# A planner that keeps apart only the streaming parts of operations at a shared port, and a GpSimd that waits one VectorE operation earlier

## The chip, the cores and the metric

The kernel runs on one core of one Trainium2 chip. The metric is device time in microseconds of one execution, as a median over runs. The engines are named as the profile names them: PE (TensorE), ACT (ScalarE), DVE (VectorE), POOL (GpSimd), SP (SyncE, which only issues DMAs here).

## The reference

Two layers, each of attention and a feed-forward block, over 2048 rows of width 448 in bf16, with residuals:

```python
def _A_ref(x, wqkv, wo):                       # H = 16 heads, Dh = 28
    q, k, v = (x @ wqkv) split into heads
    scores = jnp.einsum("bhqd,bhkd->bhqk", q, k) * scale
    p = _softmax(scores, axis=-1)
    return (p @ v, heads joined) @ wo
def _B_ref(x, w1, b1, w2, b2):                 # F = 1792
    h = x @ w1 + b1
    return jnp.where(h > 0, h, 0) ** 2 @ w2 + b2
x = x + _A_ref(_layernorm(x), ...)
x = x + _B_ref(_layernorm(x), ...)
x = x + _A_ref(_layernorm(x), ...)
x = x + _B_ref(_layernorm(x), ...)
```

The costly part is the softmax: 2 layers x 16 heads x 2048 x 2048 exponentials, with no subtraction of a maximum.

## The kernel before

**Tiles.** Queries are taken in blocks of 256 rows (the last two blocks of the second layer have 128), heads in groups of four. A *unit* is one head, one query block and as many key blocks as make a 128x512 tile of scores: 2048 units in all. `s_stream` (matmuls at line 993) multiplies keys with queries into a PSUM tile `sc` that holds three units; there are two such tiles. `e_stream` (line 1023) lets ScalarE take the exponential of the tile into `pt`. `p_stream` (line 1179) multiplies `pt` with the values `V_sb` and accumulates in `oT`; a column of ones in `V_sb` gives the sum of the softmax. Around it run the projections (line 721, evacuated at 740 to 772), the layer norms (562, 567, 589 and 590 on GpSimd, 684, 631), the normalisation of the attention's output (1206, 1208, 1288, 1307, or 1249 to 1265), the output projection with the residual (1317) and the feed-forward block (relu at 1375, square at 1384).

**Units that ScalarE does not do.** `apart` decides, when a tile of scores is issued, whether its third unit is handed to VectorE and GpSimd. Then ScalarE's instruction has 1024 columns instead of 1536, and the unit takes this way (`a_unit`, `a_rest`), where the exponential is built from integer parts and a parabola:

- `take`, line 1071, VectorE, PSUM to an SBUF buffer `v_w` (or a corner of `K_sb`);
- `part`, line 1088, GpSimd, the fraction of the exponent into `pd`, which is the unit's place in `pt` or a spare buffer in `V_sb`, `h` or `pd`;
- `bend`, line 1094, VectorE, squares it;
- either `whole`, line 1100, GpSimd, the integer part, and then `close`, line 1109, VectorE, adds the two in 16 bit; or `close` in one float operation, line 1118, VectorE alone.

`apart` says yes only where a buffer is free and where VectorE's queue of work, as the planner sees it, is under `PACE[step]`; the choice between 1109 and 1118 goes by `MIXT[step]`. Both are lists of 128 numbers, one for each 128th of the units.

**What sets the order.** The program's order on each engine is fixed when the kernel is built. A `Planner` holds some dozens of streams, each with a priority and a next operation (`Op`) with an estimated duration. It places at every step the operation that can start first by its estimates. On the chip each engine runs its instructions in that order, each waiting for semaphores of what it depends on. VectorE and GpSimd share a port to SBUF. An `Op` with `port=True` uses it: lines 684, 1094, 1109, 1118, 1384, 1307 on VectorE, 589/590, 1088, 1100 on GpSimd. This is how `earliest` keeps them apart (a and b are the start and end of an operation of the other engine, x the operation itself):

```python
for a, b, x in self.ports["POOL" if e == "DVE" else "DVE"]:
    if e == "DVE" and a <= s < b:
        s = b
    elif e == "POOL" and s < b and a < s + dur:
        s, after = b + PSYNC, x
```

So in the plan a VectorE operation starts when GpSimd's has ended, and the other way round. For a GpSimd operation that was put behind x the program also gets a true wait for the end of x (`behind`). For VectorE there is no such wait: on the chip it runs on, and the port decides.

Of the kernel before, what the change touches and what calls it, by code (L numbers as in the profile page):

```python
# [27 lines left out]
PENB = 0.3  # L28
# [4 lines left out]
PX = -9  # L33
# [41 lines left out]
C_PRIO = 1.6  # L75
V_PRIO = 8.5
# [17 lines left out]
PACE = (1.4, 4.0, 1.0, 3.4, 1.4, 1.4, 1.4, 1.0, 3.0, 1.0, 2.6, 1.4, 4.0, 2.2, 1.8, 3.0, 1.4, 4.0, 1.4, 1.8, 1.4, 4.0, 3.0, 3.0, 1.8, 3.0, 2.6, 2.2, 1.8, 3.0, 4.0, 1.4, 1.8, 3.4, 2.2, 3.0, 3.0, 4.0, 2.2, 3.0, 0.6, 2.6, 3.0, 1.4, 4.0, 4.0, 2.2, 3.0, 1.4, 3.0, 3.4, 2.6, 0.6, 2.6, 2.6, 0.6, 1.8, 2.2, 1.4, 2.2, 1.8, 1.8, 2.2, 4.0, 1.8, 3.0, 1.8, 2.2, 4.0, 3.4, 1.8, 2.6, 3.4, 3.4, 2.6, 1.8, 2.2, 3.4, 4.0, 3.4, 3.0, 4.0, 3.4, 3.4, 4.0, 3.0, 2.6, 1.4, 3.4, 1.8, 2.2, 1.8, 3.4, 3.4, 0.6, 3.4, 2.6, 1.0, 1.8, 2.2, 2.6, 3.4, 0.6, 2.6, 3.4, 3.4, 1.0, 2.2, 3.0, 2.2, 2.2, 2.6, 1.8, 3.0, 3.0, 3.0, 2.6, 3.0, 2.2, 3.0, 3.0, 1.4, 2.6, 2.2, 2.6, 2.6, 2.6, 2.6)  # L94
MIXT = (-9.0, 1.2, 99.0, 99.0, -9.0, -9.0, -9.0, -9.0, 1.8, -9.0, -9.0, 1.2, 1.2, 1.8, -9.0, 1.8, -9.0, 1.2, -9.0, 1.2, -9.0, 1.8, 1.2, 1.2, -9.0, 1.8, 1.2, -9.0, 1.2, -9.0, 99.0, 1.8, 1.2, 1.2, -9.0, -9.0, -9.0, 1.2, 1.8, 1.2, -9.0, 1.2, 1.8, -9.0, 1.8, 1.2, 1.2, 1.2, -9.0, 1.2, -9.0, 1.8, -9.0, 1.2, 1.8, 99.0, -9.0, 1.2, -9.0, -9.0, 1.8, 1.2, -9.0, -9.0, -9.0, -9.0, -9.0, -9.0, 1.8, -9.0, 1.8, 1.2, -9.0, 1.8, 99.0, -9.0, 1.8, 1.2, -9.0, 1.8, 1.8, 99.0, 99.0, 99.0, 99.0, 1.2, -9.0, 99.0, 1.8, 1.8, 1.2, -9.0, 1.8, -9.0, 1.2, -9.0, 1.8, -9.0, 1.8, 1.2, 1.8, -9.0, -9.0, -9.0, 99.0, 1.8, -9.0, -9.0, 1.2, 1.2, 1.8, 1.8, -9.0, -9.0, 1.2, -9.0, 1.2, 1.8, 1.8, 1.8, 1.2, -9.0, 1.8, 1.2, 99.0, 99.0, 99.0, 99.0)
# [44 lines left out]
class Op:  # L140
    __slots__ = ("eng", "dur", "fn", "deps", "acq", "rel", "mode", "sets", "start", "end", "res", "turn", "ready", "lat", "need", "got", "more", "room", "port", "base", "w", "after", "ins", "durs")

    def __init__(self, eng, dur, fn, deps=(), acq=None, rel=None, mode="full", sets=(), lat=0.0, need=1, port=False):
# [7 lines left out]
        self.w = self.after = self.ins = self.durs = None  # L151
# [5 lines left out]
class Planner:  # L157
# [3 lines left out]
    def __init__(self):  # L161
        self.clock = {"PE": 0.0, "ACT": 0.0, "DVE": 0.0, "POOL": 0.0, "DMA": 0.0, "-": 0.0}
        self.mode = None
        self.tok = {}
        self.streams = []
        self.past = {"PE": [], "DVE": []}
        self.used = []
        self.ports = {"POOL": [], "DVE": []}
        self.turns = lambda: False
        self.slack = lambda: SLACK  # L170

    def behind(self, late, soon):
# [18 lines left out]
    def earliest(self, o):  # L191
# [20 lines left out]
        for e in o.eng:  # L212
# [16 lines left out]
    def run(self):  # L229
        while self.streams:  # L230
# [14 lines left out]
            free = min((c[0] for c in known if c[2] == "DVE" and not c[3][2].port and c[3][2].dur > 0.2), default=1e9)  # L245
            pool = min((c[0] for c in known if c[2] == "POOL" and c[3][2].port), default=1e9)
            locked = min((c[0] for c in known if c[2] == "DVE" and c[3][2].port), default=1e9)

            def key(c):
# [4 lines left out]
                return c[0] + (PENB if held else PENA if wait else 0.0), c[1]  # L254
# [20 lines left out]
            if o.port and e in self.ports:  # L275
                self.ports[e] = [*self.ports[e][-5:], (s, o.end, o)]
# [16 lines left out]
def kernel(  # L293
# [134 lines left out]
    def sums():  # L428
# [20 lines left out]
        def split(e):  # L449
            nc.vector.tensor_copy(out=cs[:, 0:NFC], in_=box["t"][:, 0:NFC])  # L450
            nc.vector.tensor_tensor(out=cs[:, NFC:2 * NFC], in0=box["t"][:, 0:NFC], in1=cs[:, 0:NFC], op=ALU.subtract)
# [50 lines left out]
    def wprep():  # L502
        def cp(dst, c0, h0, h1):
            def fn(e):
# [4 lines left out]
                else:  # L509
                    nc.vector.tensor_copy(out=d, in_=src)  # L510
# [46 lines left out]
    def stats(mv, t0, j, deps, src=None, rel=None):  # L557
        box = {}

        def take(e):  # L560
            box["st"] = sp.tile([P, 6], DT.float32, name="st")
            nc.vector.bn_stats(out=box["st"][:, :], in_=x_sb[:, t0 + j, :] if src is None else src())  # L562

        def merge(e):
            if mv[0] is None:
                mv[0] = sp.tile([P, 4, 2], DT.float32, name="mv")
            nc.vector.bn_aggr(out=mv[0][:, j, :], in_=box["st"][:, :])  # L567
# [5 lines left out]
    def layernorm(t0, nt, deps_of, early=False, mv=None, place=None, x_in=None, parts=False):  # L573
# [9 lines left out]
        for a, b in [(0, 1), (1, 2)] if single else [(0, nt)]:  # L583
# [8 lines left out]
            rs = Op("POOL", 0.95, rsqrt, deps=[mv[1][b - 1]], sets=[("rs", t0 + a)] if early else (), port=True)  # L592
            rss += [rs] * (b - a)
            pl.spawn(EV, iter([rs]))
            if not parts and NORMG and not early:
                def turned(e, a=a, b=b):
                    ln["m"] = mv[0][:, 2:4, 0]
                    nc.vector.tensor_scalar(out=ln["m"][:, a:b], in0=mv[0][:, a:b, 0], scalar1=-1.0, scalar2=None, op0=ALU.mult)
# [12 lines left out]
        def turn(p0, own, xs):  # L611
# [13 lines left out]
            def ev(e, p0=p0, w=len(xs) * P):  # L625
# [4 lines left out]
                else:  # L630
                    nc.vector.tensor_copy(out=dst, in_=tp[:, :, 0:w])  # L631
# [4 lines left out]
        if parts:  # L636
# [4 lines left out]
            for lo, hi in ((0, 2 * P), (2 * P, D)):  # L641
                def norm(e, lo=lo, hi=hi):
                    nc.vector.tensor_scalar(out=xn[:, lo:hi], in0=x_sb[:, t0, lo:hi],
# [6 lines left out]
            for h, nm in enumerate(nms):  # L650
# [11 lines left out]
                def ev(e, h=h):  # L662
                    nc.vector.tensor_copy(out=xnT[:, 2 * h:2 * h + 2, 0:P], in_=box["t"][:, 2 * h:2 * h + 2, 0:P])
# [6 lines left out]
        for p0 in range(0, nt, wide):  # L670
# [4 lines left out]
            for j in js:  # L675
# [12 lines left out]
                nm = Op("POOL" if on else "DVE", GN if on else 0.39, norm, deps=[rss[j], *([] if x_in is None else [x_in])], sets=[("n", t0, j)] if early else (), port=True)  # L688
# [45 lines left out]
    def copy_to(dst, by=None):  # L734
        def f(e, t):
# [3 lines left out]
            elif by is not None:  # L739
                nc.vector.tensor_scalar(out=dst, in0=src, scalar1=by, scalar2=None, op0=ALU.mult)  # L740
            elif e == "ACT":
                nc.scalar.copy(out=dst, in_=src)
            else:
                nc.vector.tensor_copy(out=dst, in_=src)
        return f

    def qkv(l, t0, nt, xnT, own_xt, ends, early=False):
# [13 lines left out]
        def values():  # L761
            nonlocal last
            for tb in range(t0, t0 + nt):
                if l == 1:
                    yield Op("POOL", 0.2, lambda e, tb=tb: nc.gpsimd.memset(V_sb[1][:, tb, :, DH:DHP], 1.0))
                def evv(e, t, tb=tb):
# [4 lines left out]
                    else:  # L771
                        nc.vector.tensor_copy(out=o, in_=i)
# [99 lines left out]
    step = [0]  # L872
# [54 lines left out]
    def s_stream():  # L927
        while at[0] < len(units):
# [5 lines left out]
            def fn(e, gi=gi, us=us, js=js):  # L934
# [19 lines left out]
                else:  # L954
# [18 lines left out]
                    pl.spawn(C_PRIO, a_unit(gi, x, dst[-1], us[-1], passes[us[0][0]][0]))  # L973
# [90 lines left out]
    def a_unit(gi, x, src, unit, l):  # L1064
# [3 lines left out]
        def take(e):  # L1068
# [4 lines left out]
            if x is gbuf[gi]["s"]:  # L1073
                apart_from(gi, t)
        c = Op("DVE", 0.69, take, deps=[("s", gi)], acq=sets_of(unit), rel=x)
# [3 lines left out]
        pl.spawn(lambda now: V_LAST if e_now[1] - gi >= V_AGE or at[0] > ends_at[unit[0]] + V_PAST else V_LATE if now > c.end + V_WAIT else V_PRIO if gi > FIRST else V_FIRST, a_rest(gi, c, box, unit))  # L1079

    def a_rest(gi, c, box, unit):
# [7 lines left out]
        y = Op("POOL", GY, part, deps=[c, ("p", gi)] if own else [c], acq=None if own else lambda: pd_free(unit), port=True, lat=YL)  # L1089
# [5 lines left out]
        h = Op("DVE", 0.42, bend, deps=[y], port=True)  # L1095
        gbuf[gi]["x"] = y
        if left[0] > MIXT[step[0]]:
# [3 lines left out]
            z = Op("POOL", GZ, whole, deps=[y], port=True, lat=YL)  # L1101
# [8 lines left out]
            yield Op("DVE", 0.42, close, deps=[h, z], rel=c, sets=("x", gi), port=True, lat=XL)  # L1110
# [9 lines left out]
        yield Op("DVE", 0.683, close, deps=[h], rel=c, sets=("x", gi), port=True, lat=XL)  # L1120
# [7 lines left out]
    def p_stream():  # L1128


        for pi, (l, qb, g, kbs, first, last) in enumerate(passes):
# [65 lines left out]
            def ev(e, box=box, first=first, last=last, g=g, res=res, n=n, l=l, qb=qb):  # L1197
# [7 lines left out]
                if first:  # L1205
                    nc.vector.tensor_copy(out=dst, in_=src)
                else:
                    nc.vector.tensor_tensor(out=dst, in0=src, in1=part(l, qb, g), op=ALU.add)
# [30 lines left out]
    def norm_turn(l, qb, g, oe, pass_box):  # L1239
# [7 lines left out]
        def turn(e):  # L1247
            box["t"] = rp.tile([P, 2, QR], DT.float32, name="rec")
            nc.vector.transpose(out=box["t"][:, 0, 0:n], in_=pass_box["t"][:, 0:n])
# [3 lines left out]
        def rcp(e):  # L1253
            box["r"] = sp.tile([P, QR // DHP], DT.float32, name="rq")
            nc.vector.reciprocal(out=box["r"][:, 0:n // DHP], in_=halves(box["t"][:, 0, 0:n])[:, :, DH])
# [405 lines left out]
```

## Time and profile before

| | |
|---|---|
| Median of 3 runs | 826.27 us (825.02 to 827.38) |
| The profiled execution's own time | 825.07 us |
| Its span, first to last instruction | 823.3 us |
| Mean granted clock of TensorE | 0.992 |
| Busy: PE / DVE / ACT / POOL | 778.8 / 771.6 / 803.8 / 387.2 us |

A group row of the profile reads: line, engine, operation, what it writes and reads, shapes, count, then busy time and mean duration in ns, then the idle time just before, with who ended it. A window row gives busy time and count for PE, weight loads, DVE, ACT and POOL, then the granted clock, the DMAs' share and GB/s. A timeline row gives start, duration and the instruction.

### The profile page before, as it was taken

What the parts mean: (1) busy time and instruction counts of PE and PEld (TensorE: products, weight loads), DVE (VectorE), ACT (ScalarE), POOL (GpSimd) and SP (SyncE); (2) the same over time, 40 slices, a digit from 0 to 9 for tenths busy, and PEclk for the clock granted to TensorE, in tenths of its full rate; (3) what the DMA queues carried; (4) which work ended last, traced back from release to release, by engine and by line L of the source; (5) the groups of instructions that cost most, each with busy time, mean ns of one, the idle gap of its engine ahead of it and who ended that gap; (6) DMA issues with size and microseconds to landing.
All of it is one profiled execution on the core that took longest, in us unless ns stands there. A gap on an engine that the chain in (4) does not pass through costs nothing.

```text
span 823.3 us, 27379 instructions
## 1 busy us (share of the span) xinstructions
PE 778.8 (95%) x11410; PEld 402.7 (49%) x11410; DVE 771.6 (94%) x1722; ACT 803.8 (98%) x699; POOL 387.2 (47%) x654
## 2 busy tenths in 40 slices
PE   8999999999999999999999999988999999999997
PEld 4444545444545444454444544434454544445665
DVE  6999999999999999999999999899999999999965
ACT  7999999999999999999999999999999999999994
POOL 3244554655554465545445436344644545465500
PEclk9999999999999999999999999799999999999999
DMA  9200000000000000000000000011000000000000
GB/s 257 70 2 2 21 24 15 15 16 16 4 13 15 16 15 16 9 9 15 2 2 2 2 2 3 11 35 29 27 16 21 21 27 27 10 20 15 21 14 13
DMA packets 32364, 17.92 MB, mean 22 GB/s; under 512 B 17833, under 2 KB 31787, under 8 KB 32240
## 3 DMA queue, kind: packets, MB, share of 16 engines
q1 hardware_dynamic: 32240, 16.18, 7.0%
q8 instruction: 89, 1.46, 0.7%
q14 instruction: 35, 0.29, 0.1%
HBM read 13.88 MB, written 2.07 MB: 19 GB/s over the span
## 4 chain that ended last, share of the span: by engine, by line
ACT 34%; PE 30%; DVE 24%; issue 10%; POOL 1%; DMA 0%; ACTq 0%; DVEq 0%; POOLq 0%
ACT pt L1023 34%; PE mt L721 13%; PE sc L993 10%; PE oT L1179 5%; DVE v_w L1071 4%; DVE r L1375 3%; DVE pt L1109 2%; DVE pt L1094 2%; DVE x_sb L1317 1%; DVE K_sb L1071 1%; DVE st L562 1%; DVE V_sb L1109 1%; DVE V_sb L1094 1%; DVE V_sb L1384 1%; PE sc L721 1%
## 5 line engine op out<-in xcount | busy, mean ns | idle before, releaser
L1023 ACT ACTIVATE pt<-sc 128x1536 bf16<-128x1536 f32 (+1 forms) x683 | 793.0, 1374 | 3.8 <-PE sc L993 3.1
L993 PE MATMUL sc<-Q_sb,K_sb 32*128 32x256 bf16 (+1 forms) x4436 | 279.7, 267 | 29.2 <-ACT pt L1023 20.8
L993 PEld LDWEIGHTS <-K_sb 32*128 32x128 bf16 x4436 | 107.8, 92 | 205.3 <-issue 135.0
L1100 POOL TENSOR_SCALAR v_w<-v_w 128x512 int16<-128x512 f32 x191 | 121.3, 635 | 94.0 <-DVE pt L1109 25.0
L1179 PE MATMUL oT<-pt,V_sb 128*32 128x256 bf16 (+1 forms) x3996 | 157.3, 270 | 0.9 <-ACT pt L1023 0.5
L1071 DVE TENSOR_SCALAR v_w<-sc 128x512 f32<-128x512 f32 x213 | 144.8, 682 | 6.5 <-PE sc L993 5.3
L721 PE MATMUL mt<-xnT,w 128*128 128x256 bf16 (+1 forms) x896 | 119.7, 271 | 4.1 <-DVE xnT L631 1.9
L1179 PEld LDWEIGHTS <-V_sb 128*32 128x32 bf16 x4352 | 89.9, 96 | 54.7 <-issue 44.8
L721 PEld LDWEIGHTS <-w 128*128 128x128 bf16 x896 | 75.0, 97 | 39.1 <-issue 30.4
L1088 POOL TENSOR_SCALAR pt<-v_w 128x512 bf16<-128x512 uint16 x94 | 58.8, 626 | 51.0 <-PE sc L993 9.5
L1375 DVE TENSOR_SCALAR r<-mt 128x512 bf16<-128x512 f32 x108 | 73.5, 682 | 4.4 <-PE mt L721 4.2
L1088 POOL TENSOR_SCALAR V_sb<-v_w 128x512 bf16<-128x512 uint16 x75 | 46.3, 617 | 55.0 <-DVE V_sb L1109 12.8
L721 PE MATMUL mt<-w,V_sb 128*128 128x448 bf16 (+1 forms) x274 | 69.0, 353 | 0.0
L1100 POOL TENSOR_SCALAR K_sb<-K_sb 128x512 int16<-128x512 f32 x72 | 46.0, 639 | 36.9 <-DVE h L1109 6.2
L1071 DVE TENSOR_SCALAR K_sb<-sc 128x512 f32<-128x512 f32 x84 | 57.3, 682 | 4.1 <-PE sc L993 3.3
L1094 DVE TENSOR_TENSOR pt<-pt 128x512 bf16<-128x512 bf16 x130 | 57.7, 459 | 1.1 <-POOL pt L1088 1.1
L589 POOL TENSOR_TENSOR ve<-mv,eps_t 128x2 f32<-128x2 f32 (+1 forms) x33 | 6.4, 194 | 77.1 <-DVE mv L567 39.7
L1094 DVE TENSOR_TENSOR V_sb<-V_sb 128x512 bf16<-128x512 bf16 x93 | 40.1, 435 | 0.5 <-POOL V_sb L1088 0.5
L1317 DVE TENSOR_TENSOR x_sb<-x_sb,mt 128x448 bf16<-128x448 bf16 x61 | 37.2, 610 | 3.3 <-PE mt L721 3.2
L1109 DVE TENSOR_TENSOR pt<-pt,v_w 128x512 int16<-128x512 bf16 x88 | 38.8, 451 | 1.1 <-POOL v_w L1100 0.2
L562 DVE BATCH_NORM_STATS2 st<-x_sb 128x6 f32<-128x448 bf16 x63 | 38.4, 615 | 1.1 <-DMA x_sb<-in_A_x_dram 0.7
L1088 POOL TENSOR_SCALAR pt<-K_sb 128x512 bf16<-128x512 uint16 x36 | 22.3, 618 | 32.7 <-DVE K_sb L1071 6.4
(151 smaller groups left out, 925.3 us busy)
## 6 DMA issues: line engine op xcount, KB each, us to landing
rec<-scr SPq DMA_DIRECT2D x54, 128.0 KB
x_sb<-in_A_x_dram SPq DMA_DIRECT2D x8, 224.0 KB
out_dram<-x_sb SPq DMA_DIRECT2D x15, 112.0 KB
w<-in_B_w_dram SPq DMA_DIRECT2D x1, 1568.0 KB
w<-in_B_w_dram SPq DMA_DIRECT2D x1, 1344.0 KB
dn<-oT_sb SPq DMA_DIRECT2D x54, 4.0 KB
V_sb<-in_A_wqkv_dram SPq DMA_DIRECT2D x4, 168.0 KB
scr<-dn SPq DMA_DIRECT2D x27, 8.0 KB
```

The costliest lines, as they stand in the source:

```text
L562: nc.vector.bn_stats(out=box["st"][:, :], in_=x_sb[:, t0 + j, :] if src is None else src())
L721: nc.tensor.matmul(box["t"][:, c0:c0 + n], lhsT=lhsT() if callable(lhsT) else lhsT, rhs=rhs, start=a, stop=b)
L993: nc.tensor.matmul(dst[k][:, i * nt * P:(i + 1) * nt * P], lhsT=K_sb[l][rows, g, (kb + i) * P:(kb + i + 1) * P], rhs=Q_sb[rows, g, t0 * P: ...
L1023: t = nc.scalar.activation(out=pt[:, 0:n], in_=gbuf[gi]["sc"][:, 0:n], func=AF.Exp, scale=float(np.log(2.0)) * 2.0 ** -FRAC)
L1071: t = nc.vector.tensor_scalar(out=box["w"], in0=two(src), scalar1=EXP_SHIFT, scalar2=EXP_LOW, op0=ALU.add, op1=ALU.max)
L1088: return nc.gpsimd.tensor_scalar(out=two(pd), in0=low, scalar1=-EXP_MID * 65536, scalar2=EXP_BEND, op0=ALU.add, op1=ALU.mult)
L1094: return nc.vector.tensor_tensor(out=pd, in0=pd, in1=pd, op=ALU.mult)
L1100: return nc.gpsimd.tensor_scalar(out=two(box["t"]), in0=box["w"], scalar1=EXP_BITS, scalar2=1.0, op0=ALU.add, op1=ALU.mult)
L1109: return nc.vector.tensor_tensor(out=pd.bitcast(DT.int16), in0=pd, in1=box["t"], op=ALU.add)
L1179: nc.tensor.matmul(box["t"][DHP * hh:DHP * hh + DHP, 0:n], lhsT=V_sb[l][:, kb + i, 4 * g + hh, :], rhs=p[:, c0:c0 + n], start=begin and kb ...
L1317: nc.vector.tensor_tensor(out=x_sb[:, tb, lo:hi], in0=x_sb[:, tb, lo:hi], in1=t[:, 0:hi - lo], op=ALU.add)
L1375: nc.vector.tensor_scalar(out=r[:, 0:w], in0=t[:, 0:w], scalar1=0.0, scalar2=None, op0=ALU.max)
```

## The change

1. `port` may now be a number or a pair: the last so many microseconds of the operation, or from and to after its start. VectorE's 16-bit operations (1094, 1109, 1384) hold the port for their last 0.27 us (`LW`) of 0.42, the float ones (1118, 1307) for 0.537 (`LX`), the layer norm's (684) for 0.128 (`LN`); GpSimd's exponential steps for the last 0.477 (`LG`) of 0.617. `earliest` keeps only these parts apart.
2. A GpSimd operation that follows VectorE's x no longer waits for the end of x but for the end of the VectorE operation just ahead of x, provided that x follows that one within 0.03 us in the plan (`PNEXT`). To know it, each VectorE operation now returns its instruction.
3. `PACE` and `MIXT` have new numbers (mean of `PACE` 2.49, now 2.62; the entry of `MIXT` that forbids the second GpSimd step, 99.0, 15 times, now 5 times). Three more constants become lists of 128 equal entries with the old value (`HELD` 0.3, `OPENS` 1.6, `RESTS` 8.5).

```diff
+    def locks(self, o, e, s):
+
+        end = s + (o.dur if o.durs is None else o.durs[e])
+        return (end - o.port, end) if not isinstance(o.port, tuple) else (s + o.port[0], s + o.port[1])
...
             if o.port and e in self.ports:
-                dur = o.dur if o.durs is None else o.durs[e]
                 for a, b, x in self.ports["POOL" if e == "DVE" else "DVE"]:
-                    if e == "DVE" and a <= s < b:
-                        s = b
-                    elif e == "POOL" and s < b and a < s + dur:
-                        s, after = b + PSYNC, x
+                    lo, hi = self.locks(o, e, s)
+                    if lo < b and a < hi:
+                        s += b - lo
+                        if e == "POOL":
+                            after = x
+                            if x.prev is None or x.prev.end + PNEXT < x.start:
+                                s = max(s, x.end + PSYNC)
...
                 if e == "POOL" and o.after and o.after.eng == ("DVE",):
-                    self.behind(o.ins, o.after.ins)
+                    x = o.after
+                    self.behind(o.ins, (x if x.prev is None or x.prev.end + PNEXT < x.start else x.prev).ins)
...
             if o.port and e in self.ports:
-                self.ports[e] = [*self.ports[e][-5:], (s, o.end, o)]
+                self.ports[e] = [*self.ports[e][-5:], (*self.locks(o, e, s), o)]
+            if e == "DVE" and o.fn and o.ins:
+                o.prev, self.last = self.last, o
...
-        h = Op("DVE", 0.42, bend, deps=[y], port=True)
+        h = Op("DVE", 0.42, bend, deps=[y], port=LW)
...
-            z = Op("POOL", GZ, whole, deps=[y], port=True, lat=YL)
+            z = Op("POOL", GZ, whole, deps=[y], port=LG, lat=YL)
...
-        yield Op("DVE", 0.683, close, deps=[h], rel=c, sets=("x", gi), port=True, lat=XL)
+        yield Op("DVE", 0.683, close, deps=[h], rel=c, sets=("x", gi), port=LX, lat=XL)
```

The planner comes to another order almost everywhere, so the two programs can only be compared by counts. From their lists of instructions:

| instructions of the built program | before | after |
|---|---|---|
| ACT exponential, 1536 columns / 1024 columns | 385 / 298 | 368 / 315 |
| DVE `take` (1071) | 297 | 314 |
| POOL `part` (1088) / POOL `whole` (1100) | 297 / 263 | 314 / 291 |
| DVE `bend` (1094) | 297 | 314 |
| DVE `close` in 16 bit (1109) / in float (1118) | 263 / 34 | 291 / 23 |
| places on DVE with one port operation between others | 132 | 221 |
| SP, all | 187 | 187 |

After the change a line stands about 20 further down (1023 becomes 1043, 1094 becomes 1116).

More of the change, by code (lines that the diff above doesn't have):

```diff
@@ L32 @@
 PSYNC = 0.08
-PX = -9
+PNEXT = 0.03
+LW = 0.27
+LX = 0.537
+LG = 0.477
+LN = 0.128
+LR = (0.1, 0.3)
+PX = -9.0
 GZ = 0.617
@@ L140 @@
 class Op:
-    __slots__ = ("eng", "dur", "fn", "deps", "acq", "rel", "mode", "sets", "start", "end", "res", "turn", "ready", "lat", "need", "got", "more", "room", "port", "base", "w", "after", "ins", "durs")
+    __slots__ = ("eng", "dur", "fn", "deps", "acq", "rel", "mode", "sets", "start", "end", "res", "turn", "ready", "lat", "need", "got", "more", "room", "port", "base", "w", "after", "ins", "durs", "prev")
     def __init__(self, eng, dur, fn, deps=(), acq=None, rel=None, mode="full", sets=(), lat=0.0, need=1, port=False):
@@ L170, in __init__ @@
         self.slack = lambda: SLACK
+        self.step = [-1]
+        self.last = None
     def behind(self, late, soon):
@@ L245, in run @@
             free = min((c[0] for c in known if c[2] == "DVE" and not c[3][2].port and c[3][2].dur > 0.2), default=1e9)
+            k = self.step[0]
+            hold = HELD[k] if k >= 0 else 0.3
             pool = min((c[0] for c in known if c[2] == "POOL" and c[3][2].port), default=1e9)
@@ L871 @@
     left = [0.0]
-    step = [0]
+    step = pl.step
     def sets_of(unit):
@@ L1088, in part @@
             return nc.gpsimd.tensor_scalar(out=two(pd), in0=low, scalar1=-EXP_MID * 65536, scalar2=EXP_BEND, op0=ALU.add, op1=ALU.mult)
-        y = Op("POOL", GY, part, deps=[c, ("p", gi)] if own else [c], acq=None if own else lambda: pd_free(unit), port=True, lat=YL)
+        y = Op("POOL", GY, part, deps=[c, ("p", gi)] if own else [c], acq=None if own else lambda: pd_free(unit), port=LG, lat=YL)
         yield y
@@ L1205, in ev @@
                 if first:
-                    nc.vector.tensor_copy(out=dst, in_=src)
+                    return nc.vector.tensor_copy(out=dst, in_=src)
                 else:
-                    nc.vector.tensor_tensor(out=dst, in0=src, in1=part(l, qb, g), op=ALU.add)
+                    return nc.vector.tensor_tensor(out=dst, in0=src, in1=part(l, qb, g), op=ALU.add)
             if last and (l, qb, g // 2) not in pairs:
@@ L1308, in mul @@
                                     in1=box["r"][:, :, 0:n], op=ALU.mult)
-        m = Op(("DVE", "POOL"), 0.13 + 2 * n / 930, mul, deps=[r, oTn_of[l, qb][1]], rel=pair["own"], port=True)
+        m = Op(("DVE", "POOL"), 0.13 + 2 * n / 930, mul, deps=[r, oTn_of[l, qb][1]], rel=pair["own"], port=LX)
         m.durs = {"DVE": 0.13 + 2 * n / 930, "POOL": 0.2 + 2 * n * 1.075 / 512}
@@ L1388, in then @@
                 pool = GS_ON and f0 // pack % GS_ON == 1 and len(units) - at[0] > GS_STOP
-                b["s"] = Op("ACT" if aside else "POOL" if pool else "DVE", 0.5 if aside else GS if pool else 0.42, square, deps=[o], rel=o, port=True)
+                b["s"] = Op("ACT" if aside else "POOL" if pool else "DVE", 0.5 if aside else GS if pool else 0.42, square, deps=[o], rel=o, port=LW)
                 return [b["s"]]
```

78 lines of the change are left out of this document (40 added, 38 removed).

## The prediction, on record before the changed kernel ran

> **What bounds the kernel now.** I read first the page's table of busy times, then the chain that ended last, then the windows, then the groups of ScalarE, VectorE and GpSimd by form, the waits, and last the timeline at two places where the two engines that share a port meet.
>
> ```profile
> span 823.3 us, 27379 instructions
> PE 778.8 (95%) x11410; PEld 402.7 (49%) x11410; DVE 771.6 (94%) x1722; ACT 803.8 (98%) x699; POOL 387.2 (47%) x654
> ACT 34%; PE 30%; DVE 24%; issue 10%; POOL 1%; DMA 0%; ACTq 0%; DVEq 0%; POOLq 0%
> ```
>
> Three engines are nearly full, and the chain changes between them, so an average over the span does not say which one has to give. The windows do (columns: stretch, its length, then busy time of PE, weight loads, DVE, ACT, POOL, then the granted clock):
>
> ```profile
> 0.00:12.70 12.70, 9.32 (x55) 5.33 (x55) 6.80 (x29) 8.29 (x12) 5.78 (x16) 0.87 0.83 236
> 12.70:782.00 769.30, 733.42 (x10593) 373.06 (x10590) 740.13 (x1626) 766.13 (x663) 380.11 (x635) 0.99 0.07 19
> 782.00:808.00 26.00, 24.46 (x625) 16.00 (x624) 16.85 (x43) 26.00 (x21) 0.80 (x3) 1.00 0.04 12
> 808.00:823.30 15.30, 11.56 (x147) 8.34 (x146) 7.79 (x27) 3.33 (x6) 0.56 (x1) 1.00 0.06 17
> ```
>
> From 12.7 us to 808 us ScalarE is idle for 3.2 us in all (769.30 less 766.13, and nothing in the stretch behind). The head of 12.7 us and the end of 15.3 us contain almost none of the softmax. So the time is head + ScalarE's work + end, as long as the others keep up. In the long middle stretch VectorE is idle for 29.2 us, PE for 35.9 us, GpSimd for half of the time.
>
> ```profile
> ACT pt L1023 <- PE sc L993: 3.1, 9, 0.6
> PE sc L993 <- ACT pt L1023: 20.8, 61, 0.9
> ```
>
> Of PE's idle time 20.8 us is spent waiting for ScalarE's exponentials to free a score buffer. PE would go faster if ScalarE did; it is not the limit.
>
> **Part one: what leaves ScalarE.** The lists of instructions of the two built programs say what the planner now decides. The 683 exponentials (line 1023) stay 683, but 17 of them lose a third of their width: 385 of 1536 columns and 298 of 1024 become 368 and 315. Each of these hands one tile of 128x512 scores to VectorE and GpSimd.
>
> ```profile
> L1023 ACT ACTIVATE pt<-sc 128x1536 bf16<-128x1536 f32 x385 | 556.1, 1562 | 3.1 <-PE sc L993 2.6
> L1023 ACT ACTIVATE pt<-sc 128x1024 bf16<-128x1024 f32 x298 | 312.9, 1130 | 0.6 <-PE sc L993 0.5
> ```
>
> 17 x (1562 - 1130 ns) = 7.3 us less on ScalarE. All of it lies on the path, because ScalarE has no idle time that could swallow it. One evacuation in the head moves to VectorE, and one squaring near the end comes to ScalarE:
>
> ```profile
> L742 ACT CAST K_sb<-sc 128x512 bf16<-128x512 f32 x1 | 0.6, 585 | 0.9 <-PE sc L721 0.9
> L1382 ACT ACTIVATE V_sb<-r 128x256 bf16<-128x256 bf16 x1 | 0.4, 416 | 0.0
> ```
>
> They lie outside the middle and go in opposite directions, so I take the pair at nothing (0.6 us either way if only one of them counts).
>
> **Part two: what VectorE takes on.** The same lists show on VectorE 17 more evacuations of scores (line 1071), 17 more squarings of the exponential's fraction (1094), 28 more closing additions in 16 bit (1109) and 11 fewer closing operations in float (1118), since more units use GpSimd for the second step too. DMAs are the same in number and SyncE's list is equally long.
>
> ```profile
> L1071 DVE TENSOR_SCALAR v_w<-sc 128x512 f32<-128x512 f32 x213 | 144.8, 682 | 6.5 <-PE sc L993 5.3
> L1118 DVE SCALAR_TENSOR_TENSOR pt<-v_w,pt 128x512 int16<-128x512 f32 x6 | 4.1, 686 | 0.1
> 398.74 0.46 DVE L1109 TENSOR_TENSOR pt<-pt,v_w 128x512 int16<-128x512 bf16 x1
> 399.12 0.41 DVE L1094 TENSOR_TENSOR V_sb<-V_sb 128x512 bf16<-128x512 bf16 x1
> ```
>
> The third row ends at 399.20 and the fourth starts at 399.12: records of neighbours overlap by 0.08 us, so an instruction occupies VectorE for its duration less 0.08. That gives 17 x 0.60 + 17 x 0.33 + 28 x 0.34 - 11 x 0.61 = 10.2 + 5.6 + 9.5 - 6.7 = 18.6 us more. VectorE's middle becomes 740.1 + 18.6 = 758.7 us of work. ScalarE's middle plus its 3.2 us of idle becomes 769.3 - 7.3 = 762.0 us. So VectorE would have to run at 99.6% to let the whole gain through. This is where the prediction is decided. GpSimd gets 45 more operations of 0.62 us, 28 us on top of 380 in a stretch of 762: no limit.
>
> **Part three: the port.** The same lists with their semaphore values show what GpSimd's exponential steps wait for. Before, some 240 of them wait for the end of a VectorE operation that uses the port (1094, 1109, 1118, 1384, 684, 1307). After, 320 of them wait for an operation whose successor uses the port, and start beside that successor; behind it comes an operation that does not use the port. The pattern exists in the trace already, where two port operations stood in a row. There VectorE's row at 399.12, just quoted, is the successor, and GpSimd's is this:
>
> ```profile
> 399.36 0.66 POOL L1100 TENSOR_SCALAR v_w<-v_w 128x512 int16<-128x512 f32 x1 [0.43 <-DVE pt L1109]
> 400.09 0.62 POOL L1088 TENSOR_SCALAR pd<-v_w 128x512 bf16<-128x512 uint16 x1
> ```
>
> GpSimd starts 0.16 us after the operation ahead has ended (399.20), while VectorE's 1094 runs to 399.53 undisturbed in 0.41 us; GpSimd pays 0.04 us (0.66 against 0.62). Waiting for 1094 itself would have started it at 399.53 + 0.16 = 399.69. So the second half of the change gains GpSimd 0.33 us each time and costs VectorE nothing, provided that VectorE's operation starts on time. The opposite order looks like this:
>
> ```profile
> 415.11 0.62 POOL L1088 TENSOR_SCALAR pd<-v_w 128x512 bf16<-128x512 uint16 x1
> 415.43 0.57 DVE L1094 TENSOR_TENSOR pt<-pt 128x512 bf16<-128x512 bf16 x1
> ```
>
> GpSimd is first and ends at 415.73; VectorE's operation ends at 416.00, 0.27 us later, though alone it takes 0.41. So its first 0.14 us ran beside GpSimd and only the last 0.27 stood behind the port. The planner's new figure for these operations (the 0.27 that it keeps apart) is this row's. The Trainium skill, "SBUF — State Buffer", section "SBUF: two separate sides", says that the shared pair is an exclusive lock which whoever starts first holds "for the whole instruction". Read so, VectorE would have ended at 416.14; the row says otherwise, and I go by the row.
>
> Such meetings already cost something, visible as means above 0.415 us:
>
> ```profile
> L1094 DVE TENSOR_TENSOR pt<-pt 128x512 bf16<-128x512 bf16 x130 | 57.7, 459 | 1.1 <-POOL pt L1088 1.1
> L1094 DVE TENSOR_TENSOR V_sb<-V_sb 128x512 bf16<-128x512 bf16 x93 | 40.1, 435 | 0.5 <-POOL V_sb L1088 0.5
> L1109 DVE TENSOR_TENSOR pt<-pt,v_w 128x512 int16<-128x512 bf16 x88 | 38.8, 451 | 1.1 <-POOL v_w L1100 0.2
> L1384 DVE TENSOR_TENSOR V_sb<-r 128x512 bf16<-128x512 bf16 x68 | 32.3, 481 | 0.8
> ```
>
> 130 x 0.044 + 93 x 0.020 + 88 x 0.036 + 68 x 0.066 = 5.7 + 1.9 + 3.2 + 4.5 = 15 us; the smaller groups add some. What the change makes of this no row shows. Its bounds: gone (-15 us of VectorE's work), or doubled by more GpSimd operations and tighter placing (+15). GpSimd operations that wait for no port operation, and so may come first, become fewer (from about 317 to 275 by the lists), and on VectorE a port operation with none beside it becomes more frequent (132 such places, then 221), so that GpSimd can stream under the longer operation behind it (0.60 to 0.68 us against 0.62). I take -3 us: a fifth of 15, between the two bounds and nearest to no change.
>
> **The sum.** VectorE's middle: 758.7 - 3 = 755.7 us. How full can it be? These stretches have ScalarE wholly busy:
>
> ```profile
> 52.70:72.70 20.00, 19.63 (x277) 10.21 (x275) 19.90 (x44) 20.00 (x18) 8.77 (x15) 1.00 0.01 2
> 312.70:332.70 20.00, 19.36 (x267) 9.61 (x265) 19.96 (x44) 20.00 (x19) 10.73 (x19) 1.00 0.06 16
> 200.00:300.00 100.00, 96.30 (x1368) 48.72 (x1357) 97.71 (x214) 99.77 (x88) 52.36 (x90) 1.00 0.05 14
> ```
>
> VectorE at 99.5% to 99.8% starves nobody for 20 us; over 100 us the most that is seen is 97.7%. I take 99%, near the first two, because the planner spreads the 17 units evenly over the run: 755.7 / 0.99 = 763.3 us, 6.0 less than 769.3. The profiled execution took 825.07 us (span 823.3 and 1.8 around it), and stands 1.2 under the median of the three runs; 825.07 - 6.0 = 819.1, as a median **820 us**.
>
> **The rivals.** (a) *VectorE becomes the bound.* It cannot be kept at 99% over 769 us, only at the 97.71% of the busiest 100 us. Then the middle is 758.7 / 0.9771 = 776.5, 7.2 longer than before, and the median 833.5. This is slower, though ScalarE has less to do: evacuations of scores (1071) queue behind port operations, PE gets its buffer late, ScalarE waits for PE. It decides as soon as VectorE's idle share, now 3.8%, cannot fall below what 758.7 of work in 769.3 leaves, which is 1.4%. For it: 97.7% is the most in any hundred. Against: the stretches at 99.5% and more. Chance 0.22. (b) *The two effects cancel:* idle near 1.4%, time within 0.3% (2.5 us, about what a measurement of this kernel can tell from no change), 826. Chance 0.14. (c) *GpSimd wins the race* where VectorE's port operation starts late, because it waits for GpSimd itself or for PE. Each loss costs up to 0.62 - 0.14 = 0.48 us of VectorE; at one in eight of 320, 40 x 0.4 = 16 us; (758.7 + 16) / 0.9771 = 793, and 850 us. Against: the row at 399.12, where VectorE was ahead by a good 0.2 us. Chance 0.04. (d) *Both operations hold the port for their whole duration*, so that keeping only a part of each apart puts them into each other: 0.14 us more for each meeting; 15 us at 0.15 us each (the row at 415.43) are 100 meetings, so 14 us on VectorE, and by the working of (c) 848 us. This is what the skill's page would make of it. Against: the row at 415.43. Chance 0.02. That the change does nothing is excluded by the lists.
>
> **How the numbers follow.** My forecast, ScalarE's saving passes at least by half, has 0.58. Faster 0.58; same 0.14; slower 0.22 + 0.04 + 0.02 = 0.28. The low end is the whole 7.3 us and ScalarE's 3.1 us of waiting for PE gone: 826.27 - 10.4 = 816, and 815 with rounding of the end. The high end is (a), 834 rounded up; (c) and (d) are left out. The forecast's own range is 815 to 823.
>
> **What would show it.** Right: exponentials busy 7 us less with ScalarE's idle time in the middle still under 5 us; VectorE above 98% there, its total near 780 to 787 us; the means of lines 1094 and 1109 (moved by the new lines) not above 0.46; GpSimd's rows starting about 0.16 us after the operation ahead. Wrong: ScalarE idle 10 us or more, waiting for PE, and PE waiting for VectorE's evacuations of scores (case a); or means of 0.50 and more at the squarings and closings (c, d).

## The result, and the profile after

The changed kernel takes 819.56 us (median of 4 runs, 819.41 to 820.90) against 825.64 us of the kernel before on the same chip: ratio 0.9927, 95% interval 0.9907 to 0.9947. It is 0.7% faster, by 6 us, and the interval excludes 1. The profiled execution took 819.42 us.

The head of the page of the changed kernel:

```profile
span 817.5 us, 27550 instructions
PE 774.1 (95%) x11400; PEld 398.2 (49%) x11400; DVE 776.2 (95%) x1773; ACT 797.6 (98%) x699; POOL 447.1 (55%) x699
ACT pt L1043 25%; PE mt L741 15%; PE sc L1013 11%; PE oT L1201 5%; DVE v_w L1091 5%; DVE r L1397 3%; DVE pt L1131 2%; DVE pt L1116 2%; DVE K_sb L1091 2%; DVE st L582 1%; DVE x_sb L1339 1%; DVE V_sb L1116 1%; DVE oTn L1329 1%; DVE V_sb L1131 1%; DVE Q_sb L760 1%
```

ScalarE is busy for 6.2 us less than before (803.8), VectorE for 4.6 us more (771.6), GpSimd for 60 us more (387.2). The chain leads through ScalarE's exponentials for 25% of the span where it was 34%. Two stretches of the windows, in the columns used above; the changed kernel reaches 802 where the one before reached 808, so 776 stands for 782:

```profile
12.70:776.00 763.30, 727.55 (x10561) 367.73 (x10561) 743.43 (x1673) 757.99 (x662) 440.16 (x681) 0.99 0.07 19
776.00:802.00 26.00, 24.96 (x625) 16.46 (x624) 16.22 (x43) 25.86 (x21) 0.74 (x2) 1.00 0.05 15
```

By these windows the 6 us come out of the long middle stretch (769.3, now 763.3). VectorE there is idle for 19.9 us instead of 29.2, ScalarE for 5.3 instead of 3.2. But 12.70 us is where the first exponential of the kernel before starts. In the changed kernel it starts 2.0 us earlier, so a part of the 6 us belongs to the head:

```profile
12.70 1.45 ACT L1023 ACTIVATE pt<-sc 128x1536 bf16<-128x1536 f32 x1 [0.61 <-PE sc L993]
10.69 2.79 ACT L1043 ACTIVATE pt<-sc 128x1536 bf16<-128x1536 f32 x2 [0.61 <-PE sc L1013]
```

Most of these 2.0 us need not be the change's. From 8 to 12.7 us TensorE's granted clock was 0.66 in the profile before and 1.00 in this one. Two of the experiments below have it the other way round: `u_before` (the planner before, clock 1.00 there) starts its exponentials at 11.11 us, `d1_no_wait` (the changed order, clock 0.67 there) at 12.25 us. By these pairs the changed head is some 0.4 us shorter at like clocks. The clock is not the whole of it, since `f_lock`, in the changed order, starts at 12.21 us at a clock of 1.00. From the start of the first exponential to the end of the last the profile has 796.2 us before and 792.4 us after, 3.8 us less; the end behind it takes 14.4 us in both.

The groups by form that answer to the rows shown before, with GpSimd's largest group before as the first row:

```profile
L1100 POOL TENSOR_SCALAR v_w<-v_w 128x512 int16<-128x512 f32 x191 | 121.3, 635 | 94.0 <-DVE pt L1109 25.0 <-DVE V_sb L1109 12.9 <-DVE pt L1094 9.9
L1043 ACT ACTIVATE pt<-sc 128x1536 bf16<-128x1536 f32 x368 | 532.1, 1544 | 3.6 <-PE sc L1013 3.0
L1043 ACT ACTIVATE pt<-sc 128x1024 bf16<-128x1024 f32 x315 | 325.9, 1120 | 2.5 <-PE sc L1013 1.5 <-POOL v_w L1122 0.8
L1116 DVE TENSOR_TENSOR pt<-pt 128x512 bf16<-128x512 bf16 x138 | 61.7, 457 | 0.2 <-POOL pt L1110 0.2
L1116 DVE TENSOR_TENSOR V_sb<-V_sb 128x512 bf16<-128x512 bf16 x96 | 39.9, 420 | 0.0
L1131 DVE TENSOR_TENSOR pt<-pt,v_w 128x512 int16<-128x512 bf16 x91 | 38.7, 430 | 1.4 <-POOL v_w L1122 0.5
L1406 DVE TENSOR_TENSOR V_sb<-r 128x512 bf16<-128x512 bf16 x67 | 28.2, 423 | 0.1
L1122 POOL TENSOR_SCALAR v_w<-v_w 128x512 int16<-128x512 f32 x206 | 137.2, 666 | 61.9 <-DVE pt L1131 14.5 <-DVE pd L1131 4.6 <-DVE pt L1116 3.8
```

The four VectorE rows are the same four groups as in the prediction. Above 0.415 us they hold 138 x 0.042 + 96 x 0.005 + 91 x 0.015 + 67 x 0.008 = 5.8 + 0.5 + 1.4 + 0.5 = 8 us, where it was 15. Summed over every port operation on VectorE (its duration less that of an undisturbed one of its kind, negative where it is shorter) the waits at the port are 27.0 us before and 18.6 us after. GpSimd's row went from 635 to 666 ns, and its idle time before these operations from 94.0 to 61.9 us: it now spends inside the operation a part of what it spent at a semaphore.

### The profile page after: what moved, and what is told of

It reads as the page before. It is cut to its first block, busy times and chain, and to the rows that moved or that the text cites. A ratio compares the mean times of both kernels' runs of the same rounds, so it can differ in the third digit from the quotient of the medians.

```text
span 817.5 us, 27550 instructions
## 1 busy us (share of the span) xinstructions
PE 774.1 (95%) x11400; PEld 398.2 (49%) x11400; DVE 776.2 (95%) x1773; ACT 797.6 (98%) x699; POOL 447.1 (55%) x699
## 4 chain that ended last, share of the span: by engine, by line
PE 34%; DVE 29%; ACT 26%; issue 8%; POOL 3%; DMA 1%; SPq 0%; ACTq 0%; DVEq 0%; POOLq 0%
ACT pt L1043 25%; PE mt L741 15%; PE sc L1013 11%; PE oT L1201 5%; DVE v_w L1091 5%; DVE r L1397 3%; DVE pt L1131 2%; DVE pt L1116 2%; DVE K_sb L1091 2%; DVE st L582 1%; DVE x_sb L1339 1%; DVE V_sb L1116 1%; DVE oTn L1329 1%; DVE V_sb L1131 1%; DVE Q_sb L760 1%
## 5 line engine op out<-in xcount | busy, mean ns | idle before, releaser
L1043 ACT ACTIVATE pt<-sc 128x1536 bf16<-128x1536 f32 (+1 forms) x683 | 786.9, 1348 | 6.1 <-PE sc L1013 4.5
L1013 PE MATMUL sc<-Q_sb,K_sb 32*128 32x256 bf16 (+1 forms) x4430 | 280.5, 267 | 29.7 <-ACT pt L1043 19.9
L1122 POOL TENSOR_SCALAR v_w<-v_w 128x512 int16<-128x512 f32 x206 | 137.2, 666 | 61.9 <-DVE pt L1131 14.5
L1091 DVE TENSOR_SCALAR v_w<-sc 128x512 f32<-128x512 f32 x225 | 152.1, 680 | 3.8 <-PE sc L1013 3.5
L1110 POOL TENSOR_SCALAR pt<-v_w 128x512 bf16<-128x512 uint16 x99 | 65.2, 658 | 64.1 <-DVE v_w L1091 34.1
L1110 POOL TENSOR_SCALAR V_sb<-v_w 128x512 bf16<-128x512 uint16 x73 | 50.0, 684 | 50.4 <-DVE v_w L1091 14.0
L1122 POOL TENSOR_SCALAR K_sb<-K_sb 128x512 int16<-128x512 f32 x85 | 58.4, 687 | 26.9 <-DVE pt L1116 4.1
L741 PE MATMUL mt<-w,V_sb 128*128 128x448 bf16 x274 | 69.9, 355 | 0.0
L1116 DVE TENSOR_TENSOR pt<-pt 128x512 bf16<-128x512 bf16 x138 | 61.7, 457 | 0.2 <-POOL pt L1110 0.2
L609 POOL TENSOR_TENSOR ve<-mv,eps_t 128x2 f32<-128x2 f32 (+1 forms) x33 | 10.5, 319 | 57.2 <-DVE mv L587 42.5
L1110 POOL TENSOR_SCALAR pt<-K_sb 128x512 bf16<-128x512 uint16 x39 | 25.9, 665 | 20.3 <-DVE K_sb L1091 8.3
```

The source lines that it names most:

```text
L741: nc.tensor.matmul(box["t"][:, c0:c0 + n], lhsT=lhsT() if callable(lhsT) else lhsT, rhs=rhs, start=a, stop=b)
L1013: nc.tensor.matmul(dst[k][:, i * nt * P:(i + 1) * nt * P], lhsT=K_sb[l][rows, g, (kb + i) * P:(kb + i + 1) * P], rhs=Q_sb[rows, g, t0 * P: ...
L1043: t = nc.scalar.activation(out=pt[:, 0:n], in_=gbuf[gi]["sc"][:, 0:n], func=AF.Exp, scale=float(np.log(2.0)) * 2.0 ** -FRAC)
L1091: t = nc.vector.tensor_scalar(out=box["w"], in0=two(src), scalar1=EXP_SHIFT, scalar2=EXP_LOW, op0=ALU.add, op1=ALU.max)
L1110: return nc.gpsimd.tensor_scalar(out=two(pd), in0=low, scalar1=-EXP_MID * 65536, scalar2=EXP_BEND, op0=ALU.add, op1=ALU.mult)
L1116: return nc.vector.tensor_tensor(out=pd, in0=pd, in1=pd, op=ALU.mult)
```

## The experiments

In all tables of this section the ratio is to the kernel before, on the same chip, with its 95% interval; the changed kernel stands at 0.9927.

**The waits alone, order kept.** In `c1_wait_x` each of GpSimd's port waits goes back to the operation that it follows, in `d1_no_wait` the port waits are left out; the order of instructions on every engine is that of the changed kernel.

```diff
-                    self.behind(o.ins, (x if x.prev is None or x.prev.end + PNEXT < x.start else x.prev).ins)
+                    self.behind(o.ins, x.ins)        # c1_wait_x; d1_no_wait: pass
```

> The changed kernel in the same order of instructions, but each of GpSimd's true port waits goes back to the end of the VectorE operation that it follows, instead of the one ahead. Nothing else differs: 314 units off ScalarE. Theory one (ScalarE's work sets the time, GpSimd has slack): some 320 GpSimd operations start 0.33 us later, GpSimd is idle for 45% of the span, so at most 1 us is lost: 819.5 to 821. Theory two (the earlier start carries the gain, since the plan now counts on it and VectorE's squarings and closings follow closely): GpSimd streams 0.33 us later than planned and meets the next port operation, 320 x 0.1 us on a VectorE that is 97% full: 826 or more.

> The changed kernel in the same order, with none of the waits that exist for the port alone; waits for data stay. GpSimd starts as soon as its data are there, and the port decides. Theory one (the order of the plan does the work): GpSimd is at times first, VectorE's mean for the 16-bit operations goes from 0.43 to about 0.48 us, 700 operations x 0.05 = 35 us, of which VectorE has some 20 us of room: 825 to 835. Theory two (the waits are of no use, the port settles it fairly): 818 to 821, with VectorE's means unchanged.

| | us | ratio | VectorE busy | its waits at the port |
|---|---|---|---|---|
| changed kernel | 819.56 | 0.9927 [0.9907, 0.9947] | 776.2 | 18.6 |
| c1_wait_x | 850.61 | 1.0322 [1.0303, 1.0341] | 809.5 | 53.0 |
| d1_no_wait | 869.77 | 1.0548 [1.0521, 1.0574] | 832.6 | 77.0 |

Theory one, that GpSimd has slack and a start 0.33 us later costs next to nothing, is refuted by 30 us. The same place in both kernels shows why: first VectorE and GpSimd in the changed kernel, then in `c1_wait_x`. The squaring (1116) uses the port, the copy (651) does not, the closing (1131) does. The first row (x2) holds two closings that follow each other.

```profile
118.20 0.74 DVE L1131 TENSOR_TENSOR V_sb<-V_sb,K_sb 128x512 int16<-128x512 bf16 x2
118.87 0.41 DVE L1116 TENSOR_TENSOR pt<-pt 128x512 bf16<-128x512 bf16 x1
119.20 0.68 DVE L651 COPY xnT<-tp 128x1024 bf16<-128x1024 bf16 x1
119.80 0.41 DVE L1131 TENSOR_TENSOR pt<-pt,v_w 128x512 int16<-128x512 bf16 x1
119.10 0.66 POOL L1122 TENSOR_SCALAR v_w<-v_w 128x512 int16<-128x512 f32 x1 [0.95 <-DVE V_sb L1131]
```

```profile
119.32 0.41 DVE L1116 TENSOR_TENSOR pt<-pt 128x512 bf16<-128x512 bf16 x1
119.66 0.68 DVE L651 COPY xnT<-tp 128x1024 bf16<-128x1024 bf16 x1
120.26 0.52 DVE L1131 TENSOR_TENSOR pt<-pt,v_w 128x512 int16<-128x512 bf16 x1
119.89 0.62 POOL L1122 TENSOR_SCALAR v_w<-v_w 128x512 int16<-128x512 f32 x1 [1.29 <-DVE pt L1116]
```

With the early wait GpSimd starts 0.16 us after the operation ahead (118.20 + 0.74 = 118.94), loses 0.04 us to the squaring, and is done at 119.76, before the closing begins. With the late wait it starts 0.16 us after the squaring (119.73), streams until 120.51 and holds up the closing by 0.11 us. The copy between is not long enough to hide a GpSimd operation that starts 0.23 us into it.

The traces show how often each case occurs, if every port operation on VectorE is set against its undisturbed length (0.415 us in 16 bit, 0.68 in float, 0.39 for the layer norm's). In the changed kernel GpSimd starts beside a VectorE port operation that is already under way in 262 places, and in 260 of them VectorE's operation keeps its length. Before the change there were 43 such places, in `c1_wait_x` there are 30. Instead GpSimd is there first, and VectorE's operation is longer than undisturbed by more than 0.025 us, in 262 places of `c1_wait_x` and in 94 of the changed kernel, by 0.21 us on average in both.

VectorE's waits at the port rose by 34.4 us, its busy time by 33.3, the span by 33.2 (to 850.7). Without any port wait the three numbers are 58.4, 56.4 and 52.0. So VectorE's lost time passes into the span almost one for one. Its idle time is the same in the changed kernel and in `c1_wait_x` (41.3 and 41.2 us of the span), so the loss is not VectorE waiting for results that come later. The mean granted clock was lower (0.992, 0.984 and 0.980 in the three profiles), but the four executions of `c1_wait_x`, from 849.39 us at 0.990 to 852.68 us at 0.984, put only some 3 us on that. `d1_no_wait` took the way of theory one, VectorE's means of the first groups rising to 0.48 to 0.54 us, but 35 us beyond the upper end of its range: the 20 us of room on VectorE that it counted on were none.

Twenty of the 33 us of `c1_wait_x` end in the waits of ScalarE; the row below stood at 4.5 us in the changed kernel. They reach it through TensorE, whose weight loads for the scores wait 54.0 us for VectorE's evacuations into `v_w` (line 1091), 24.1 us in the changed kernel.

```profile
ACT pt L1043 <- PE sc L1013: 24.4, 57, 1.6
```

**Which engine sets the time.** `s_act` repeats a third of 18 exponentials on ScalarE, `s_dve` repeats 18 evacuations of the feed-forward block on VectorE. Order and waits are otherwise those of the changed kernel.

```diff
+                    if whole_n[0] % 20 == 10:      # s_act, behind a full exponential
+                        nc.scalar.activation(out=pt[:, 0:512], in_=gbuf[gi]["sc"][:, 0:512], func=AF.Exp, ...)
...
+                    if relu_n[0] % 6 == 3:         # s_dve, ahead of the same instruction
+                        nc.vector.tensor_scalar(out=r[:, 0:w], in0=t[:, 0:w], scalar1=0.0, scalar2=None, op0=ALU.max)
```

> The changed kernel, order kept, with 18 short exponentials of 512 columns repeated on ScalarE (every twentieth full tile), 18 x (0.43 + 0.06) = 8.8 us more on ScalarE and nothing elsewhere. Theory one (ScalarE's work sets the time): 819.5 + 8.8 = 828, of which at most the 5 us of ScalarE's idle time could absorb a part: 825 to 829. Theory two (VectorE is the bound now): 820 to 823. Theory three (the interleaving of VectorE and GpSimd sets it, any disturbance costs more than its length): 832 or more.

> The changed kernel, order kept, with 18 of the 108 evacuations of the feed-forward block (0.68 us, occupying 0.60) done twice on VectorE, 10.8 us more on VectorE and nothing elsewhere. Theory one (ScalarE sets the time, VectorE has 20 us of idle time in the middle): 820 to 823. Theory two (VectorE is the bound): 828 to 831. Theory three (interleaving: the repeats shift VectorE against GpSimd, port meetings follow): 832 or more.

`s_act` took 827.52 us, ratio 1.0029 [1.0017, 1.0040]; `s_dve` 828.84 us, ratio 1.0046 [1.0030, 1.0061]. Against the changed kernel's ratio that is 0.0102 and 0.0119 of 825, 8.4 and 9.8 us. By the profiles ScalarE was busy 10.0 us longer in the first (807.6) and VectorE 11.3 us longer in the second (787.5). Both theories that name one engine alone fail, and the 832 us of theory three are not reached either: each engine passes on about 85% of what it is given (84% and 87%, each uncertain by a fifth, since the changed kernel's own ratio is from another chip). The idle time of the loaded engine in the middle does not shrink: ScalarE has 4.9 us in `s_act`, VectorE 19.6 us in `s_dve`, against 5.3 and 19.9. VectorE's 19.9 us lie in 127 gaps, the longest of 2.0 us, and 11.0 us of them end with PE; that this is why they absorb nothing was not tried. The windows of the middle, first `s_act`, then `s_dve`, show the other engine merely stretched (745.57 and 760.71 us, against 743.43 and 757.99):

```profile
12.70:785.00 772.30, 730.47 (x10560) 370.84 (x10560) 745.57 (x1673) 767.41 (x679) 439.15 (x681) 0.99 0.07 19
```

```profile
12.70:786.00 773.30, 729.89 (x10563) 366.95 (x10560) 753.73 (x1690) 760.71 (x662) 438.75 (x681) 0.99 0.07 18
```

**Planner or lists.** `a1_old_lists` is the changed planner with the old `PACE` and `MIXT`, `b1_new_lists` the planner before with the new ones.

> The changed planner with the two lists of 128 numbers (PACE, MIXT) of the kernel before; it hands 303 units to VectorE and GpSimd (before 297, changed 314). Theory one (time follows ScalarE's work): 6 x 0.43 = 2.6 us less than before, 823. Theory two (the lists fit only the planner for which they were chosen): units come at the wrong places, ScalarE waits, 826 to 832. Theory three (the planner alone is the gain): 819 to 820.

> The planner and the waits of the kernel before, with the new lists; 298 units off ScalarE. Theory one (time follows ScalarE's work): 825, as before. Theory two (lists fit only their own planner): 828 to 834. Theory three (the new lists are the gain, whatever the planner): 819 to 821.

834.47 us, ratio 1.0121 [1.0105, 1.0137], and 860.72 us, 1.0429 [1.0403, 1.0454]. Either half without the other is slower than the kernel before: the lists fit only the planner for which they stand, as theory two had it, though the first is 2 us and the second 27 us beyond what it allowed. So no run with borrowed lists can say what the planner is worth. The next ones use lists that belong to neither.

```diff
+PACE = (2.6,) * 128                                 # u_before_low, u_after_low: 2.2
+MIXT = (1.2,) * 128
...
-                            if x.prev is None or x.prev.end + PNEXT < x.start:
-                                s = max(s, x.end + PSYNC)
+                            s = max(s, x.end + PSYNC)            # u_locks_only, with self.behind(o.ins, x.ins)
```

> The changed planner with PACE 2.6 and MIXT 1.2 for all 128 steps, so lists that fit neither planner; 306 units off ScalarE. To be set beside the same lists in the planner before (300 units). Theory of the planner (the planner itself is better, whatever the lists): 822 to 832 and some 5 us less than the other. Theory of the lists (lists found for a planner make the time): 835 to 855, about as long as the other.

> The planner and the waits of the kernel before with PACE 2.6 and MIXT 1.2 for all steps; 300 units off ScalarE. The changed planner with these lists took 832.6. Theory of the planner: 5 us or more above that, 838 to 850. Theory of the lists (two planners without lists of their own are alike): 830 to 836.

> The first half of the change alone, with the same uniform lists: only the streaming parts are kept apart, but a GpSimd operation behind a VectorE operation waits for the end of that one, in the plan and on the chip; 304 units off ScalarE. Theory of the locks (the truer port carries the planner's gain): 831 to 834, as the whole change. Theory of the wait (the second half carries it): as the planner before, 838 to 850.

> The planner and the waits of the kernel before with PACE 2.2 and MIXT 1.2 for all steps; 290 units off ScalarE. A second pair for the same question, since one pair could be chance. Theory of the planner: 5 us or more above its partner. Theory of the lists: within 3 us of its partner.

> The changed planner and waits with PACE 2.2 and MIXT 1.2 for all steps; 304 units off ScalarE, 14 more than its partner. Theory of the planner: 826 to 834 and 5 us or more below its partner. Theory of the lists: within 3 us of its partner.

| uniform lists | planner before | locks only | whole change |
|---|---|---|---|
| `PACE` 2.6 | 845.85, 1.0260 [1.0228, 1.0291] | 849.94, 1.0305 [1.0288, 1.0322] | 832.63, 1.0088 [1.0063, 1.0114] |
| `PACE` 2.2 | 838.44, 1.0155 [1.0130, 1.0180] | not run | 827.89, 1.0036 [1.0020, 1.0053] |

With equal lists the changed planner is 1.7% and 1.2% better, 13 and 11 us, with 6 and 14 more units off ScalarE (at 0.43 us each 2.6 and 6.0 us of it). The theory of the planner stands, though `u_after` lies 0.6 us above its range. The half of it that keeps apart only the streaming parts brings nothing by itself (1.0305 against 1.0260). I read this so, and did not try it further: as long as GpSimd waits for the end of the operation that it follows, a finer plan of the port gains no place to put it. The streaming parts alone were tried with one pair of lists only, and a plan is a single sample.

**Holding GpSimd to the plan.** `f_lock` gives the remaining GpSimd port operations a wait that is already over in the plan.

```diff
+                elif e == "POOL" and o.port:
+                    y = self.last
+                    while y is not None and y.end + 0.16 > o.start:
+                        y = y.prev
+                    if y is not None:
+                        self.behind(o.ins, y.ins)
```

> The changed kernel, same order, where also those GpSimd port operations that had no port wait get one: for the last VectorE operation that the plan has finished 0.16 us before their start. In the plan this costs nothing; on the chip it keeps GpSimd from running ahead. The remaining lock waits of VectorE in the changed kernel, some 19 us, come for the greater part from GpSimd operations without a port wait. Theory one (ScalarE sets the time): lock waits fall, time within 2 us of 819.5. Theory three (the interleaving as planned is what counts): 814 to 818, VectorE's means of the 16-bit operations at 0.42.

820.81 us, ratio 0.9933 [0.9907, 0.9959]: no difference from the changed kernel. That is the time of theory one, without the fall in waits that it named. VectorE's means stayed as well, here the first group (457 in both):

```profile
L1122 DVE TENSOR_TENSOR pt<-pt 128x512 bf16<-128x512 bf16 x138 | 61.7, 457 | 0.2 <-POOL pt L1116 0.2
```

GpSimd is still first, at VectorE's cost, in 98 places, where the changed kernel has 94. So these added waits remove nothing of what is left at the port, 18.6 us. They hold GpSimd back only by whole VectorE operations, so they do not exclude that it runs ahead by less than one; what the rest comes from stays open.

## Why the prediction was right, and where its steps were off

The forecast was 820 us with a range of 815 to 834; 819.56 was measured. The direction and the path were right: ScalarE lost exponentials, VectorE took them on without slowing the kernel. That the number agrees within 0.5 us is luck. The forecast took 6.0 us out of the softmax and left the head as it was; in the profiles the softmax gave 3.8 us and the head 2.0, of which some 0.4 remain at like clocks. And within the softmax two errors cancelled, as follows.

- *ScalarE's saving, 7.3 us.* The groups of exponentials went from 793.0 to 786.9 us busy, 6.1 less, and the idle time before them from 3.8 to 6.1, which leaves the 3.8 us of the softmax. Right in kind, 1.2 us too large. ScalarE's records overlap when it runs on without a gap; in the middle it started 22 times after a gap instead of 16, and the six lost overlaps of about 0.2 us would make up the difference. This was worked out, not tried.
- *VectorE's work, +18.6 - 3.* This is the mis-sized term. The middle holds 743.4 us of VectorE's work, not 755.7. Two things were too small: the waits at the port fell by 8.4 us, not by 3, and fuller running saves time of its own. An instruction that follows directly overlaps its predecessor by 0.08 us, one that follows a gap does not. Durations less busy time in the middle, which is the sum of these overlaps, went from 114.7 to 122.8 us, 8.1 more, where 47 more instructions at 0.08 make 3.8; that is 4.3 us. Another 1.5 us of work now lies ahead of 12.7 us (VectorE's head has 8.31 us instead of 6.80). With the 5.4 us of the waits these make 11.2 of the 12.3 us.
- *VectorE at 99%.* It ran at 97.4% of the middle (743.43 of 763.30), close to the 97.7% of rival (a), and it did not slow the kernel. The two errors cancelled: less work, lower share. But 97.7% is no ceiling, as rival (a) had it, and the 97.4% is a mean of unlike stretches. Three rows of the changed kernel, in the columns used above:

```profile
400.00:500.00 100.00, 96.42 (x1355) 48.97 (x1356) 93.37 (x202) 100.00 (x88) 52.51 (x84) 1.00 0.01 2
500.00:600.00 100.00, 91.36 (x1332) 44.16 (x1332) 95.56 (x218) 97.34 (x87) 57.50 (x85) 0.93 0.09 23
600.00:700.00 100.00, 98.28 (x1381) 48.98 (x1376) 99.09 (x223) 100.00 (x90) 60.75 (x94) 1.00 0.08 21
```

From 600 to 700 us, and in each hundred from 100 to 400, VectorE is busy for 98.5 to 99.1%, near the 99% that I took. From 400 to 500 us it has 6.6 us to spare while ScalarE has none. From 500 to 600 us the granted clock was 0.93, and both have idle time; that stretch alone holds half of ScalarE's 5.3 us (before, at 0.95, it held 1.8 of 3.2). `s_dve` shows that VectorE was already passing on most of what it was given.

- *GpSimd no limit.* It is not, but I took its start for a matter of indifference to VectorE, a gain of 0.33 us "each time" with no one who needs it. `c1_wait_x` puts 31 us on it. The planner had filled the place behind that early start with VectorE's next port operation. The gain of the second half is not that GpSimd ends sooner; it is that GpSimd's streaming fits under one VectorE operation of 0.6 to 0.7 us, and that VectorE can therefore alternate.
- *Rival (c), GpSimd first.* Did not happen: at 119.10 VectorE was ahead by 0.23 us, and 260 of the 262 VectorE operations that GpSimd joined ran undisturbed. Its price for one lost race, 0.4 us, was too high: `c1_wait_x` has 0.21 us on average, `d1_no_wait` 0.31 us. What makes the loss 50 us in `d1_no_wait` is their number, 265 operations longer by more than 0.025 us where the changed kernel has 96.
- *Rival (d), the port held for the whole operation.* Refuted on this chip: at 119.10 GpSimd started while the squaring (118.87 to 119.28) was in its streaming part, and ended 0.48 us behind it, 0.14 us less than its own 0.62. It is so throughout: where GpSimd was first and a 16-bit operation grew longer, VectorE ended 0.27 us behind GpSimd in all 86 places of the changed kernel (0.268 to 0.274) and in all 239 of `c1_wait_x` (0.266 to 0.274). The sentence of the Trainium skill ("SBUF — State Buffer", "SBUF: two separate sides") holds for the streaming part only.
- *Of the signs named beforehand:* ScalarE's idle time in the middle is 5.3 us (under 5 was named), VectorE's share of the middle is 97.4% (above 98% was named) and its total 776.2 (780 to 787 was named), and one of the named means is above 0.46 (the `pd` group of line 1116, 465 ns). GpSimd's rows start 0.16 us after the operation ahead where it releases them, as said.

## What to carry to other kernels

Where two engines share a port, the order in which they meet can be worth more than the load on either. Here the same instructions in the same order cost 31 us more when one engine was released a third of a microsecond later. Release the slower engine by the event ahead of the one that it must follow, so that its start-up runs under that operation, and leave behind it an operation that does not need the port. And a kernel whose lists were found for one planner cannot judge another planner: compare both with lists that belong to neither.

## What the runs showed of the hardware

An operation on the shared port has a part that needs the port and a part that does not: of VectorE's 0.41 us the last 0.27, of GpSimd's 0.62 the last 0.48. The float operations have 0.54 us of 0.68 with the port, the layer norm's 0.13 of 0.39, by how long they end behind a GpSimd operation that was first. When GpSimd is released by the operation ahead, a VectorE port operation that has started costs it 0.04 us if it is one in 16 bit and 0.30 us if it is one in float (GpSimd's medians 0.66 and 0.92 us beside them, 0.62 alone). A GpSimd operation that starts first cost VectorE 0.11 us in the row shown and 0.21 us on average where it cost anything; the longest of the changed kernel was 0.46 us. An idle share of 2.6% on VectorE was no reserve: about 85% of the work added in `s_dve` showed in the time.
